# Three more groups transposed by DMA instead of TensorE, and one pair of scores placed in a later tile

## The chip, the cores and the metric

One core of a Trainium2 chip runs the whole program. The metric is the device time of one execution in microseconds (us). The kernel before took 308.35 us, the median of 3 runs (308.3 to 310.02).

## What is computed

Retention (attention without a softmax, with a decay by distance) and behind it a two-layer network with a gate:

```python
scores = scale * np.matmul(q, k.transpose(0, 1, 3, 2))        # batch 8, heads 8, sequence 576, head dim 64
gamma = 1.0 - 2.0 ** (-5.0 - np.arange(H))
Dmat = np.where(rel >= 0, gamma[:, None, None] ** rel[None, :, :], 0.0)   # rel = i - j
x = np.matmul(scores * Dmat, v)                               # then as 4608 tokens x 512
h = x @ w_in                                                  # 512 -> 2048
out = (h * np.cos(h)) @ w_out                                 # 2048 -> 512
```

## The kernel before

**Groups.** The 4608 tokens are 36 groups of 128. For each group, `load` (line 97) issues three DMAs on SP's queue (q, k, v in float32); `prep` (line 123) has POOL (GpSimd) multiply q and k by powers of the decay into the bfloat16 tile `qks`, and copy v to `vb`. The scores need q and k with the head dimension on the partitions, so `transposes` (line 147) turns `qks` into `qkT`: for groups below `N_PE_T` on TensorE (eight 128x128 transposes on line 155 into PSUM banks that it is given, then two copies by ACT on line 160), for the others by one transposing DMA on SP's queue (line 150). `scores` (line 170) makes 8 score blocks and has DVE multiply them with a triangular mask into `ret` (line 186). `state` (line 194) adds the group to a running state and copies it (line 215). `attn_out` (line 223) sums the state's part and the masked scores' part in a PSUM bank and evacuates it to the transposed activations `xT` (line 260), on DVE or on ACT as the caller says.

**Tiles.** The network works on ten tiles of 512, 256, 256 and seven times 512 tokens (n = 0 to 9). `mm1` (line 264) is the first layer with ACT's cosine (line 283; a sine with a quarter period added) and DVE's product (line 284); `mm2` (line 286) is the second layer, whose result ACT copies to `ot` (line 301) and SP stores (line 303).

**Order.** The order on each engine is the order in which the program is written, by hand. In the second layer of tile n, the list `todo` says at which step of `order` (a step is one matmul of line 292) the attention of later groups is put in: a pair (50, f) means that f is issued just before step 50. `inside` does the same within the first layer. Thus group 5 has its transposes at step 61 of tile 0 and its scores inside the first layer of tile 1; groups 6 and 7 have their transposes at steps 4 and 9 of tile 1 and their scores at step 16; the scores of groups 8 and 9 come at step 11 of tile 2, those of 10 and 11 at step 25 of tile 2, those of 12 to 15 in tile 3 at steps 12 and 25, and those of 16 and 17, the first of tile 4, at step 52 of tile 3.

**Feeding.** After each store, `feed(s)` (line 308) goes on with loads, preparations and, for groups from `N_PE_T` on, transposing DMAs, as far as the conditions on lines 312 to 323 let it. All these DMAs and the stores are issued by SP in that order, so a transposing DMA whose input isn't ready holds up what is behind it. The counters start at 6 (line 431), because groups 4 and 5 have been loaded and prepared ahead of the loop.

**PSUM.** Banks a, b and m hold 1024 float32 a partition each and are shared by transposes, scores, outputs and both layers; n and st are half as large.

Of the kernel before, what the change touches and what calls it, by code (L numbers as in the profile page):

```python
# [17 lines left out]
def kernel(  # L18
# [16 lines left out]
    nc = tc.nc  # L35
# [8 lines left out]
    NG = NTOK // P  # L44
# [8 lines left out]
    widths = [512, 256, 256] + [512] * 7  # L53
    assert sum(widths) == NTOK
    starts = [sum(widths[:n]) for n in range(len(widths))]
    N_PE_T = 8

    consts = ctx.enter_context(tc.tile_pool(name="consts", bufs=1))
    first = ctx.enter_context(tc.tile_pool(name="first", bufs=1))
# [87 lines left out]
    def transposes(g, banks=None, only=(0, 1)):  # L147
        qks, vb, qkT, qT = tiles["a", g]
        if g >= N_PE_T:
            nc.sync.dma_start(qkT, qks.rearrange("s m h d -> s (m h d)"), transpose=True)  # L150
            return
        for m in only:
            ps = psum.tile([P, HG, P], BF16, tag=banks[m], name="tr")
            for hg in range(HG):
                nc.tensor.transpose(  # L155
                    ps[:, hg, :],
                    qks[:, m, 2 * hg : 2 * hg + 2, :].rearrange("s h d -> s (h d)"),
                    ident,
                )
            nc.scalar.copy(qkT[:, m * HG : (m + 1) * HG, :], ps)  # L160
        if ("fv", g) in tiles and g != 3:
            nc.scalar.copy(vb, tiles.pop(("fv", g)))
# [60 lines left out]
    def attn_out(gs, bank, evac=nc.vector.tensor_copy):  # L223


        ps = psum.tile([P, len(gs), HG, P], F32, tag=bank, name="ov")
        for x, g in enumerate(gs):
            c = g % PER
            if c == 0:
                continue  # L230
            qT = tiles["a", g][3]
            sb = tiles.pop(("sb", g))
            n = HP if c == MIX else P
            for hg in range(HG):
                nc.tensor.matmul(  # L235
                    ps[:, x, hg, :n],
                    lhsT=sb[:, hg, :],
                    rhs=qT[:, hg, :n],
                    start=(hg == 0),
                    stop=False,  # L240
                    skip_group_check=True,
                )
        for x, g in enumerate(gs):
            vb = tiles["a", g][1]
            ret = tiles.pop(("ret", g))
            for hg in range(HG):
                for he in range(2):
                    nc.tensor.matmul(  # L248
                        ps[he * D : he * D + D, x, hg, :],
                        lhsT=vb[:, 2 * hg + he, :],  # L250
                        rhs=ret[:, he, hg, :],
                        start=(g % PER == 0 and hg == 0),
                        stop=(hg == HG - 1),
                        skip_group_check=True,
                    )
        n = max(m for m in range(len(starts)) if starts[m] <= gs[0] * P)
        if ("x", n) not in tiles:
            tiles["x", n] = xp.tile([P, DG, 512], BF16, tag="xT", name="xT")
        t0 = gs[0] * P - starts[n]
        evac(  # L260
            tiles["x", n][:, :, t0 : t0 + len(gs) * P].rearrange("p c (x i) -> p x c i", i=P), ps
        )
# [43 lines left out]
    loaded = prepared = transposed = 4  # L306

    def feed(s):

        nonlocal loaded, prepared, transposed  # L310
        while True:
            while prepared < min(loaded, NG, 2 * s + 7, s + 11):
                prep(prepared)
                prepared += 1
                if transposed < N_PE_T:
                    transposed += 1

            if N_PE_T <= transposed < min(prepared, s + 11) and (
                transposed <= loaded - 2 or loaded == NG
# [108 lines left out]
            attn_out([g], "m", evac=nc.scalar.copy)  # L428
    for g in (4, 5):
        prep(g)  # L430
    loaded = prepared = transposed = 6


    def pair(g, banks, sc, av, out=None):

        mid = (sc + av) // 2
        return [
            (sc - 5, lambda: state(g)),
            (sc, lambda: (scores(g, banks[0]), scores(g + 1, banks[1]))),
            (mid, lambda: state(g + 1)),  # L440
            (av, lambda: attn_out([g, g + 1], out or banks[0])),
        ]

    def scores2(g):
        if g < NG:
            scores(g, "a")
            scores(g + 1, "b")

    late = []
    for n, w in enumerate(widths):  # L450

        if n in (0, 3):
            halves = [(h, et) for et in range(0, ET, 4) for h in range(2)]
            if n == 3:
                halves.sort()
            blocks = [(et, half * 256, 256) for half, et in halves]
        elif n == 1:
            blocks = [(et, half * P, P) for half in range(2) for et in (0, 8)]
        else:
            blocks = [(et, 0, w) for et in range(0, ET, 1024 // w)]  # L460
        banks = {0: "abmabmab", 1: "bmba", 2: "bmab", 3: "mamabmab"}.get(n, "abmabmab")
        for i, (et, c0, cw) in enumerate(blocks):

            inside = {
                (0, 0): {2: lambda: (attn_out([3], "n"), state(3))},
                (1, 0): {4: lambda: scores(5, "a")},
                (1, 1): {3: lambda: attn_out([5], "a", evac=nc.scalar.copy)},
            }.get((n, i), {})
            mm1(n, et, c0, cw, banks[i], inside)
            if (n, i) == (3, 1):  # L470
                late.pop()()

        g = starts[n] // P + w // P
        if n == 0:
            todo = [
                (45, lambda: transposes(4, "ab")),
                (49, lambda: state(4)),
                (50, lambda: scores(4, "a")),
                (57, lambda: attn_out([4], "a")),
                (61, lambda: transposes(5, "ba")),  # L480
                (63, lambda: state(5)),
            ]
        elif n == 1:
            todo = [(4, lambda: transposes(6, "mb")), (9, lambda: transposes(7, "mb"))]
            todo += pair(6, "ab", 16, 27)
        elif n == 2:
            todo = pair(g, "ab", 11, 25, "m")
            todo += [(25, lambda: scores2(g + 2)), (29, lambda: state(g + 2))]
            late += [lambda: (state(g + 3), attn_out([g + 2, g + 3], "b"))]
        elif n + 1 < len(widths):  # L490
            todo = [
                (5, lambda: state(g)),
                (12, lambda: scores2(g)) if n == 3 else (0, lambda: None),
                (
                    25 if n == 3 else 20,
                    lambda: (
                        attn_out(
                            [g, g + 1], "m", nc.scalar.copy if n == 3 else nc.vector.tensor_copy
                        ),
                        scores2(g + 2),  # L500
                    ),
                ),
                (16, lambda: state(g + 1)),
                (36, lambda: state(g + 2)),
                (52, lambda: (attn_out([g + 2, g + 3], "m"), scores2(g + 4))),
                (45, lambda: state(g + 3)),
            ]
        else:
            todo = []
        todo.sort(key=lambda u: u[0])  # L510
        order, cols = [], [(0, DM)]
        for tsi in range(w // P):
            if (n + 1, tsi + 1) == (len(widths), w // P):
                cols = [(0, DM // 2), (DM // 2, 3 * DM // 4), (3 * DM // 4, DM)]
            order += [(tsi, et, c0, c1) for c0, c1 in cols for et in range(ET)]
        if n == 0:

            part = 3 * ET // 4
            order[: 2 * ET] = [
                (tsi, et, 0, DM)  # L520
                for tsi, et in [(t, e) for e in range(part) for t in range(2)]
                + [(t, e) for t in range(2) for e in range(part, ET)]
            ]
        for i, (tsi, et, c0, c1) in enumerate(order):
            while todo and todo[0][0] <= i:
                todo.pop(0)[1]()
            mm2(n, tsi, et, c0, c1)
        assert not todo
# [30 lines left out]
```

## Time and profile before

| | before |
|---|---|
| median of the runs | 308.35 us |
| the profiled execution | 308.27 us |
| its span | 306.3 us |
| TensorE busy (PE) | 300.5 us |
| DVE, ACT, POOL busy | 175.8, 117.2, 99.0 us |
| transposes on TensorE (line 155) | 48 matmuls, 220 ns each as listed, pipelined |
| copies behind them (ACT, line 160) | 12, 588 ns each |
| transposing DMAs | 28, 4.4 us each from issue to landing |
| TensorE's granted clock | full throughout |

The span runs from the first to the last instruction of the profiled execution; the run itself is 2.0 us longer. The busy time of PE counts pipelined matmuls from start to end, so the distance from one start to the next is what an additional matmul costs. In the lists of the profile, a tile's name stands before the arrow and what it is made from behind it: `qkT<-qks` on SP's queue (SPq) is a transposing DMA, `tr<-ident,qks` on PE is a transpose on TensorE, `sc<-qkT` are scores, `h` and `o` are the two layers, `fq`, `fk` and `fv` the loads. DMA issues are listed with the time to landing, that is until the last byte's completion is signalled.

### The profile page before, as it was taken

What the parts mean: (1) busy time and instruction counts of PE and PEld (TensorE: products, weight loads), DVE (VectorE), ACT (ScalarE), POOL (GpSimd) and SP (SyncE); (2) the same over time, 40 slices, a digit from 0 to 9 for tenths busy, and PEclk for the clock granted to TensorE, in tenths of its full rate; (3) what the DMA queues carried; (4) which work ended last, traced back from release to release, by engine and by line L of the source; (5) the groups of instructions that cost most, each with busy time, mean ns of one, the idle gap of its engine ahead of it and who ended that gap; (6) DMA issues with size and microseconds to landing.
All of it is one profiled execution on the core that took longest, in us unless ns stands there. A gap on an engine that the chain in (4) does not pass through costs nothing.

```text
span 306.3 us, 5685 instructions
## 1 busy us (share of the span) xinstructions
PE 300.5 (98%) x2361; PEld 171.2 (56%) x2361; DVE 175.8 (57%) x180; ACT 117.2 (38%) x136; POOL 99.0 (32%) x123
## 2 busy tenths in 40 slices
PE   7899999999999999999999999999999999999996
PEld 3478547757588554454545554455445544554444
DVE  5776425565777746656576556755676547624610
ACT  3566234715046223631264026411651165105611
POOL 2740066634554534544533334314430000000000
PEclk9999999999999999999999999999999999999999
DMA  8999999999999999999993999189925300010012
GB/s 210 213 211 206 205 230 229 190 198 246 164 243 208 196 253 199 268 220 205 258 205 58 223 218 225 23 190 208 243 48 77 99 35 0 36 68 34 2 68 69
DMA packets 148697, 49.65 MB, mean 162 GB/s; under 512 B 138688, under 2 KB 144192, under 8 KB 148672
## 3 DMA queue, kind: packets, MB, share of 16 engines
q1 hardware_dynamic: 144448, 45.10, 78.5%
q0 software_dynamic: 4224, 4.19, 8.2%
q8 instruction: 18, 0.29, 0.4%
q14 instruction: 7, 0.06, 0.1%
HBM read 36.70 MB, written 9.44 MB: 151 GB/s over the span
## 4 chain that ended last, share of the span: by engine, by line
PE 94%; SPq 2%; DMA 2%; DVE 0%; POOL 0%; issue 0%; ACT 0%; ACTq 0%
PE h L275 41%; PE o L292 41%; PE ov L248 3%; PE sc L177 3%; PE st L206 2%; PE ov L235 2%; DMA fk<-in_k_dram 2%; SPq L109 2%; PE tr L155 1%; PE sc L168 0%; DVE xT L260 0%; POOL qks L135 0%; SPq L336 0%; ACT ot L301 0%; ACTq L301 0%
## 5 line engine op out<-in xcount | busy, mean ns | idle before, releaser
L292 PE MATMUL o<-w_out_sb,gT 128*128 128x512 bf16 (+2 forms) x608 | 134.4, 369 | 0.0
L275 PE MATMUL h<-xT,w_in_sb 128*128 128x512 bf16 (+2 forms) x832 | 127.5, 314 | 0.1
L284 DVE TENSOR_TENSOR gT<-h,cosh 128x1024 bf16<-128x1024 f32 x72 | 88.2, 1225 | 55.9 <-ACT cosh L283 55.8
L275 PEld LDWEIGHTS <-w_in_sb 128*128 128x128 bf16 x832 | 75.8, 98 | 50.4 <-issue 0.4
L283 ACT ACTIVATE cosh<-h,half_pi 128x1024 f32<-128x1024 f32 x72 | 80.2, 1113 | 52.0 <-PE h L275 52.0
L292 PEld LDWEIGHTS <-gT 128*128 128x128 bf16 x608 | 55.3, 98 | 56.2
L134 POOL TENSOR_TENSOR qks<-fq,gq 128x512 bf16<-128x512 f32 x32 | 33.3, 1042 | 104.3 <-DMA fq<-in_q_dram 102.0
L301 ACT COPY ot<-o 128x512 f32<-128x512 f32 (+2 forms) x38 | 21.4, 563 | 115.4 <-PE o L292 115.4
L135 POOL TENSOR_TENSOR qks<-fk,gk 128x512 bf16<-128x512 f32 x35 | 36.5, 1042 | 13.1 <-DMA fk<-in_k_dram 11.4
L186 DVE TENSOR_TENSOR ret<-sc,tri 128x1024 bf16<-128x1024 f32 x32 | 38.0, 1218 | 4.6 <-PE sc L177 4.5
L215 DVE TENSOR_TENSOR sb<-st,diag_105 128x512 bf16<-128x512 f32 x32 | 22.0, 687 | 27.8 <-PE st L206 27.8
L260 DVE CAST xT<-ov 128x1024 bf16<-128x1024 f32 (+1 forms) x16 | 18.5, 1158 | 23.5 <-PE ov L248 23.5
L141 POOL CAST vb<-fv 128x512 bf16<-128x512 f32 x32 | 19.5, 610 | 7.7 <-DMA fv<-in_v_dram 5.7
L206 PEld LDWEIGHTS <-qks 128*128 128x128 bf16 (+1 forms) x128 | 9.5, 98 | 7.0 <-issue 0.4
L248 PE MATMUL ov<-ret,vb 128*64 128x128 bf16 x288 | 12.1, 223 | 0.0
L206 PE MATMUL st<-vb,qks 128*128 128x128 bf16 (+1 forms) x116 | 11.2, 220 | 0.1
L177 PEld LDWEIGHTS <-qkT 64*128 64x128 bf16 x288 | 8.1, 94 | 5.0 <-ACT qkT L160 2.3
L235 PEld LDWEIGHTS <-sb 128*128 128x128 bf16 x128 | 8.3, 98 | 3.8
L160 ACT COPY qkT<-tr 128x512 bf16<-128x512 bf16 x12 | 6.6, 588 | 9.3 <-PE tr L155 9.3
L177 PE MATMUL sc<-qkT 64*128 64x128 bf16 x256 | 10.1, 218 | 0.0
L248 PEld LDWEIGHTS <-vb 128*64 128x64 bf16 x288 | 8.7, 109 | 2.0
L235 PE MATMUL ov<-qkT,sb 128*128 128x128 bf16 (+1 forms) x116 | 8.8, 216 | 0.0
(49 smaller groups left out, 57.3 us busy)
## 6 DMA issues: line engine op xcount, KB each, us to landing
out_dram<-ot SPq DMA_DIRECT2D x35, 256.0 KB, 3.1
fk<-in_k_dram SPq DMA_DIRECT2D x32, 256.0 KB, 4.8
fv<-in_v_dram SPq DMA_DIRECT2D x32, 256.0 KB, 4.9
fq<-in_q_dram SPq DMA_DIRECT2D x28, 256.0 KB, 4.1
w_in_sb<-in_moe_w_in_dram POOLq DMA_DIRECT2D x4, 512.0 KB, 8.7
w_out_sb<-in_moe_w_out_dram POOLq DMA_DIRECT2D x4, 512.0 KB, 15.9
fq_111<-in_q_dram SPq DMA_DIRECT2D x2, 512.0 KB, 4.4
fq<-in_q_dram SPq DMA_DIRECT2D x8, 128.0 KB, 3.8
```

Source lines behind the costliest of these rows:

```text
L134: nc.gpsimd.tensor_tensor(out=qks[:, 0], in0=fq, in1=tq, op=ALU.mult)
L135: (nc.vector if g == 3 else nc.gpsimd).tensor_tensor(out=qks[:, 1], in0=fk, in1=tk, op=ALU.mult)
L177: nc.tensor.matmul(ps[:, he, hg, :], lhsT=qkT[d0 : d0 + D, HG + hg, :], rhs=qT[d0 : d0 + D, hg, :], start=True, stop=True,)
L186: nc.vector.tensor_tensor(out=ret.rearrange("p a b i -> p (a b) i"), in0=ps.rearrange("p a b i -> p (a b) i"), in1=mask.unsqueeze(1).to_br ...
L206: nc.tensor.matmul(ps[:, hg, :], lhsT=qks[p0:, 1, 2 * hg : 2 * hg + 2, :].rearrange("s h d -> s (h d)"), rhs=vs[p0:, 2 * hg : 2 * hg + 2, ...
L215: nc.vector.tensor_tensor(out=sb, in0=ps, in1=diag2.unsqueeze(1).to_broadcast([P, HG, P]), op=ALU.mult,)
L235: nc.tensor.matmul(ps[:, x, hg, :n], lhsT=sb[:, hg, :], rhs=qT[:, hg, :n], start=(hg == 0), stop=False, skip_group_check=True,)
L248: nc.tensor.matmul(ps[he * D : he * D + D, x, hg, :], lhsT=vb[:, 2 * hg + he, :], rhs=ret[:, he, hg, :], start=(g % PER == 0 and hg == 0), ...
L275: nc.tensor.matmul(ps[:, j, :], lhsT=w_in_sb[:, dg, (et + j) * P : (et + j + 1) * P], rhs=xT[:, dg, c0 : c0 + w], start=(dg == 0), stop=(d ...
L283: nc.scalar.activation(cosh, ps, ACTF.Sin, bias=half_pi, scale=1.0)
L284: nc.vector.tensor_mul(gT[:, et : et + m, c0 : c0 + w], ps, cosh)
L292: nc.tensor.matmul(ps, lhsT=gT[:, et, tsi * P : (tsi + 1) * P], rhs=w_out_sb[:, et, c0:c1], start=(et == 0), stop=(et == ET - 1),)
```

## The change

The threshold `N_PE_T` goes from 8 to 5, so that groups 5, 6 and 7 are transposed by DMA; their calls of `transposes` leave the hand-written lists, and the counter `transposed` starts at 5, so that `feed` issues the DMAs. The scores of groups 16 and 17 leave step 52 of tile 3 and come at step 12 of tile 4; the outputs of these groups, with the scores of groups 18 and 19 behind them, move from step 20 to step 25 of tile 4, and their evacuation goes from DVE to ACT. In tiles 5 to 8 all stays.

```diff
-    N_PE_T = 8
+    N_PE_T = 5
...
-    loaded = prepared = transposed = 6
+    loaded = prepared = 6
+    transposed = 5
...
                 (57, lambda: attn_out([4], "a")),
-                (61, lambda: transposes(5, "ba")),
                 (63, lambda: state(5)),
             ]
         elif n == 1:
-            todo = [(4, lambda: transposes(6, "mb")), (9, lambda: transposes(7, "mb"))]
-            todo += pair(6, "ab", 16, 27)
+            todo = pair(6, "ab", 16, 27)
...
-                (12, lambda: scores2(g)) if n == 3 else (0, lambda: None),
+                (12, lambda: scores2(g)) if n in (3, 4) else (0, lambda: None),
                 (
-                    25 if n == 3 else 20,
+                    25 if n in (3, 4) else 20,
                     lambda: (
                         attn_out(
-                            [g, g + 1], "m", nc.scalar.copy if n == 3 else nc.vector.tensor_copy
+                            [g, g + 1], "m", nc.scalar.copy if n in (3, 4) else nc.vector.tensor_copy
                         ),
                         scores2(g + 2),
                     ),
                 ),
...
-                (52, lambda: (attn_out([g + 2, g + 3], "m"), scores2(g + 4))),
+                (
+                    52,
+                    lambda: (attn_out([g + 2, g + 3], "m"), scores2(g + 4 if n > 3 else NG)),
+                ),
```

`scores2(NG)` issues nothing.

## Prediction

> **What bounds the kernel now.** I read the page first, then the chain of waits, PE's waits, the timelines of PE and SP between 40 and 120 us, and the DMA view in narrow windows.
>
> ```profile
> PE 300.5 (98%) x2361; PEld 171.2 (56%) x2361; DVE 175.8 (57%) x180; ACT 117.2 (38%) x136; POOL 99.0 (32%) x123
> ...
> DMA  8999999999999999999993999189925300010012
> ...
> PE 94%; SPq 2%; DMA 2%; DVE 0%; POOL 0%; issue 0%; ACT 0%; ACTq 0%
> PE h L275 41%; PE o L292 41%; PE ov L248 3%; PE sc L177 3%; PE st L206 2%; PE ov L235 2%; DMA fk<-in_k_dram 2%; SPq L109 2%; PE tr L155 1%; PE sc L168 0%; DVE xT L260 0%; POOL qks L135 0%; SPq L336 0%; ACT ot L301 0%; ACTq L301 0%
> ```
>
> After the first 18 us TensorE sets the end: it stands on 94% of the chain and its order of work is fixed, so a matmul taken out there shortens the span by its pitch, and a wait put there lengthens it one for one. But the DMA row is just as full up to slice 21 (about 160 us): loading runs at the engines' limit there, far ahead of need, and anything added to it delays all that follows in SP's queue.
>
> PE's timeline around the fifth group's transposes and scores (columns: start, duration, engine, line, operation, count):
>
> ```profile
> 47.72 0.61 PE L155 MATMUL tr<-ident,qks 128*128 128x128 bf16 x8
> 48.16 0.59 PE L292 MATMUL o<-w_out_sb,gT 128*128 128x512 bf16 x2
> 48.59 0.39 PE L206 MATMUL st<-vb,qks 128*128 128x128 bf16 x4
> 48.82 0.38 PE L292 MATMUL o<-w_out_sb,gT 128*128 128x512 bf16 x1
> 49.03 1.06 PE L275 MATMUL h<-xT,w_in_sb 128*128 128x128 bf16 x16
> 50.02 0.40 PE L177 MATMUL sc<-qkT 64*128 64x128 bf16 x8
> ```
>
> The next work starts 0.44 us after the eight transposes start (the 0.61 includes the last one's tail): 55 ns each, without a gap. PE's timeline at the first scores whose operands come late by DMA, groups 10 and 11:
>
> ```profile
> 81.37 0.64 PE L248 MATMUL ov<-ret,vb 128*64 128x128 bf16 x16
> 81.94 0.62 PE L177 MATMUL sc<-qkT 64*128 64x128 bf16 x16
> 82.50 1.04 PE L292 MATMUL o<-w_out_sb,gT 128*128 128x512 bf16 x4
> ```
>
> SP's own timeline (issue start and length), and what the DMA view gives for the single issues at 43.11 and 74.17 us (last column: time to landing):
>
> ```profile
> 43.11 1.57 SPq L109 DMA_DIRECT2D fv<-in_v_dram  x1
> 44.73 0.99 SPq L109 DMA_DIRECT2D fq<-in_q_dram  x1
> ...
> 74.17 2.02 SPq L150 DMA_TRANSPOSE qkT<-qks  x1
> 76.24 1.29 SPq L109 DMA_DIRECT2D fq<-in_q_dram  x2
> ```
>
> ```profile
> fv<-in_v_dram SPq DMA_DIRECT2D x1, 256.0 KB, 6.1
> ```
>
> ```profile
> qkT<-qks SPq DMA_TRANSPOSE x1, 5.0
> ```
>
> So group 6's values land at 49.2 and group 11's transpose at 79.2. The latter is wanted at 82.2 (half of the 16 score matmuls after 81.94): 3.0 us of slack.
>
> **What the Trainium skill says.** TensorE: Matmul & The Clock Gate, "Wait — 56ns, not 53.3ns?": warm matmuls of 128 columns follow each other at 55.6 ns; the trace agrees (55 ns above). DMA: Bandwidth & Descriptors, "Anatomy of one DMA": "DMA engines do not wait on semaphores"; a wait sits on the issuing sequencer, so a transposing DMA whose input isn't ready blocks SP and all behind it. The trace agrees so far as SP's waits list the transposes' line as waiting for POOL (7.8 us in 8 waits). The same page, "Latency and other measured facts", gives transposing DMAs 261 GB/s in the strided case; 262,144 bytes at that rate are an estimate of 1.0 us, and the trace's landings below agree.
>
> **The change part by part.**
>
> *Removed from PE:* 3 groups x 8 transposes x 55 ns = 1.33 us, all inside stretches where PE has no gap (47.7, 58.3 and 59.9 us). The six ACT copies (588 ns each, 3.5 us) and three PSUM evacuations go too; ACT is idle for longer than that around them, so they are worth nothing. Gain 1.33 us.
>
> *Added to SP's queue:* following the feeding loop by hand, store 0 is now followed by load 6, T5 (the transposing DMA of group 5), load 7, T6; store 1 by load 8, T7, load 9, T8; from store 2 on the order is the old one. What is an extra transpose worth while the queue is full? Landing of each transpose after the landing of the transfer ahead of it, T8 to T17: 0.86, 0.93, 0.87, 1.64, 0.84, 0.95, 0.83, 0.93, 0.95, 0.90 us, mean 0.97. A second way: q loads of full groups land 4.21 us apart without transposes (46.11 to 58.75, three groups, one store) and 5.27 with (58.75 to 79.81, four groups, two stores); less 0.12 for the store share, 0.93. The bounds: 0.83 is the least seen; the last transposes, which run nearly alone, keep the engines busy for some 1.5 us. I take 0.97, so 2.9 us for three (2.5 to 4.5). Nothing takes this back in time: between 60 and 100 us SP's waits sum to 0.6 us, and it issues without a rest until 159 us.
>
> *T5's own wait.* POOL ends group 5's k product at 44.4 and SP reaches T5's place at 44.7, so SP doesn't wait. T5 lands behind group 6's values: 49.2 + 0.97 = 50.2 (bounds 50.0 and 50.7). PE wants it at 50.02 - 0.44 = 49.58. PE waits about 0.6 us (0.4 to 1.2), with the whole first-layer work of tile 1 queued behind, and ACT's cosine and DVE's product after that. Net at this point: +0.2.
>
> *T6 and T7* land at 49.2 + 0.97 + three loads at 1.1 + 0.97 = 54.5 and about five DMAs later, 59.5. Scores 6 and 7, at 62.13 before, come at 62.13 + 0.2 - 0.89 = 61.4: two us of cover. Net -0.7.
>
> *T11.* 79.2 + 2.9 = 82.1. PE now wants it at 82.2 - 0.7 = 81.5, so scores 11 wait 0.6 us; behind them stand the last seven second-layer matmuls of tile 2 and tile 3. Net 0.0. There is a disturbance: transfers of the engines' instructions (single packets of 16 KB, 1.0 to 1.3 us, the DMA view's q8) hold a landing back by about 1 us when they fall in; one stands at 79.7 us, just behind T11 before. If it falls in front of T11 now, T11 lands at 83.2 and the net is +1.0. Taking T11 between them, a little nearer the first (82.4): net +0.3.
>
> *What is late next.* T13 before 94 (wanted 102), T15 at 104.8 (wanted 107.2): cover 2.4 us. T17 moves from 113.4 to 116.3; its scores were wanted at 115.0 and would have waited 1.3 us, but they are moved into tile 4. T19 and T21 keep over 7 us. Output tiles: the copy at 113.24 needs the store that landed at 107.4, now 110.3; covered.
>
> *The moved scores of groups 16 and 17:* 16 matmuls, 0.55 us of PE both before and after: nothing. In tile 4 they stand at step 12, about 134.8, when DVE has ended the last product of that tile (134.55) and T17 has landed for 18 us. Then 2 x 1.22 us of masks on DVE must be over by the outputs at step 25; tile 3 has this very arrangement (scores 102.46, masks to 105.27, outputs 106.06, no gap in PE), so it is covered by second-layer matmuls. If that cover were gone, DVE's lateness would go to PE in full, up to 2.4 us. The evacuation at step 25 goes from DVE (1.22 us) to ACT (1.01 us), which has only store copies then; the second masks on DVE start earlier for it. Nothing.
>
> *Sum:* -1.33 + 0.6 (T5) + about 1.0 (T11) = +0.3 us on the span of 306.3. The profiled execution took 308.27, 2.0 more than its span, and the median of the runs is 308.35; so 308.6.
>
> **Rivals.** (1) *The transfers are hidden.* T5 arrives in time and T11 too, and PE keeps 1.33 us: 307.0. For it: many DMAs land early by some tenths, and PE's shift decides. Against: it needs three transposes for at most 1.5 us, 0.5 each, where none of ten took under 0.83. (2) *Slower: a transpose in the full queue costs its price alone, 1.5 us.* Place: scores 11. T11 lands at 83.7 and PE, wanting it at 81.5, waits 2.2: +1.5, 309.9. It decides from 1.0 us a transpose on, where the two waits eat the gain. For it: the nearly lone transposes and the one landing of 1.64. Against: nine of ten were under 1.0. (3) *A late queue spreads:* at 2.1 us a transpose or more, scores 7 and 15 wait as well and T11 costs over 3.5: 311.5 and above. Nothing in the landings speaks for it. That the edit does nothing can't be: the transposes leave PE in any case.
>
> **How the numbers follow.** Forecast 0.55 (307.7 to 309.3), rival 1 0.17, rival 2 0.20, rival 3 0.08. The range reaches from rival 1 past rival 2: 306.9 to 310.3. About 1%, 3 us, is what a measurement of this kernel can tell from no change. Faster by more than that isn't to be had from 1.33 us of removed work: 0.02 for what I haven't seen. Slower takes rival 3 or the tail of rival 2: 0.09. Within: 0.89.
>
> **What would show it.** Line 155 with 24 matmuls fewer; 31 transposing DMAs; T5 landing near 50.2 with PE waiting 0.4 to 1.2 us ahead of the scores at about 50.2; T11 landing at 82.1 to 83.2 with a wait of 0.5 to 1.7 us on line 177; the store after T8 issued about 3 us later than 59.71; no PE gap in tile 4. I am wrong if T5 lands before 49.6, T11 before 81.5 or after 84, or if PE waits elsewhere.

## The result, and the profile after

The changed kernel took 312.54 us (median of 6 runs, 311.5 to 314.59) against 308.33 before (also 6 runs): 1.0139 times as long, 95% interval 1.0097 to 1.0181. That is outside the predicted range of 306.9 to 310.3. Two later measurements of the same kernel on other occasions gave 1.0096 (1.0064 to 1.0128) and 1.0060 (1.0029 to 1.0091); the last corresponds to 310.2 us, inside the predicted range. The ratios leave out executions more than 1.5% above the fastest of the same kernel, the medians and ranges keep them. The changed kernel scatters far more than the kernel before: 16 of its 30 executions on the three occasions show a mean granted clock of 0.995 or less, of the kernel before 2 of 126. The profiled execution is one of the longer ones, 314.14 us with a span of 312.4, 6.1 more than before.

The page after, lines as shown of before, and the row of the granted clock:

```profile
PE 299.9 (96%) x2304; PEld 171.5 (55%) x2337; DVE 174.9 (56%) x179; ACT 115.0 (37%) x131; POOL 99.1 (32%) x123
...
PEclk9999999999869999999999999999999999999999
DMA  8999999999999999999994799559952310010012
...
PE 78%; DMA 11%; SPq 6%; issue 1%; POOL 1%; ACT 0%; DVE 0%; ACTq 0%
PE h L275 36%; PE o L292 34%; SPq L109 5%; DMA w_out_sb<-in_moe_w_out_dram 5%; DMA qkT<-qks 4%; PE ov L248 3%; PE sc L177 3%; PE ov L235 2%; PE st L206 2%; DMA fk<-in_k_dram 2%; DMA fq<-in_q_dram 1%; POOL w_in_sb L376 1%; DVE xT L260 0%; SPq L303 0%; ACT cosh L283 0%
```

Two things are new: the chain runs through `DMA qkT<-qks`, back along SP's queue as far as the weights, and TensorE's granted clock, full throughout before, dips in two slices. PE's waits after name the place:

```profile
PE sc L177 <- DMA qkT<-qks: 3.8, 2, 3.1
```

Its timeline shows the first of the two waits, ahead of the scores of group 5 (the last column is the idle time before, and what ended it), and the second, ahead of those of group 11, with what follows:

```profile
48.59 1.06 PE L275 MATMUL h<-xT,w_in_sb 128*128 128x128 bf16 x16
50.34 0.40 PE L177 MATMUL sc<-qkT 64*128 64x128 bf16 x8 [0.69 <-DMA qkT<-qks]
...
81.37 0.40 PE L177 MATMUL sc<-qkT 64*128 64x128 bf16 x8
84.87 0.61 PE L177 MATMUL sc<-qkT 64*128 64x128 bf16 x8 [3.10 <-DMA qkT<-qks]
85.81 1.49 PE L292 MATMUL o<-w_out_sb,gT 128*128 128x512 bf16 x3 [0.33 <-issue]
```

The 16 scores that stood together before (81.94) are torn apart: those of group 10 run at 81.37, those of group 11 wait until 84.87. The transposing DMA on which they wait was issued at 78.06, and the DMA view of that issue gives 6.8 us to landing, where group 11's took 5.0 before:

```profile
qkT<-qks SPq DMA_TRANSPOSE x1, 6.8
```

And after the wait everything is slow: three matmuls of 512 columns take 1.49 us together, where four took 1.04 before (82.50, in the prediction). The idle time "issue" behind the scores is no wait: the trace has six of the seven matmuls that stand there, so one record is missing. Busy times by stretch, first after, then before (columns: stretch, length, busy time and count of PE, PEld, DVE, ACT and POOL, granted clock, DMA share, GB/s):

```profile
84.20:91.00 6.80, 5.80 (x29) 3.40 (x31) 1.92 (x2) 0.59 (x1) 3.25 (x4) 0.50 1.26 193
```

```profile
84.20:91.00 6.80, 6.80 (x79) 6.00 (x78) 5.08 (x7) 2.81 (x3) 4.02 (x6) 1.00 1.17 244
```

For 6.8 us (84.2 to 91.0) TensorE was granted half its clock. The counts, 29 matmuls and 79, aren't for the same work: in the changed kernel the first 0.67 us are still the wait, and the kernel before is already further on, at shorter matmuls.

Following the same instruction through both timelines gives the account (a wait costs a little more than its idle time, because the last matmul before it runs out first). Scores 5 start at 50.34 (before 50.02): 0.44 us of removed transposes and 0.76 lost waiting. Scores 6 start at 61.56 (62.13): another 0.89 saved, net -0.57, and the same at scores 10 (81.37, 81.94). Scores 11 start at 84.87 where they would have started at 81.59: 3.3 us lost, net +2.7. The outputs in tile 3 start at 94.14 (88.50): net +5.6, so the half clock cost 2.9 us. To the last matmul 0.1 more comes in, and 0.4 at the very end of the program (last section). The sum: -1.33 + 0.76 + 3.3 + 2.9 + 0.1 + 0.4 = +6.1.

### The profile page after: what moved, and what is told of

Its sections match the earlier page's. It is cut to its first block, busy times and chain, and to the rows that moved or that the text cites. A ratio compares the mean times of both kernels' runs of the same rounds, so it can differ in the third digit from the quotient of the medians.

```text
span 312.4 us, 5604 instructions
## 1 busy us (share of the span) xinstructions
PE 299.9 (96%) x2304; PEld 171.5 (55%) x2337; DVE 174.9 (56%) x179; ACT 115.0 (37%) x131; POOL 99.1 (32%) x123
## 4 chain that ended last, share of the span: by engine, by line
PE 78%; DMA 11%; SPq 6%; issue 1%; POOL 1%; ACT 0%; DVE 0%; ACTq 0%
PE h L275 36%; PE o L292 34%; SPq L109 5%; DMA w_out_sb<-in_moe_w_out_dram 5%; DMA qkT<-qks 4%; PE ov L248 3%; PE sc L177 3%; PE ov L235 2%; PE st L206 2%; DMA fk<-in_k_dram 2%; DMA fq<-in_q_dram 1%; POOL w_in_sb L376 1%; DVE xT L260 0%; SPq L303 0%; ACT cosh L283 0%
## 5 line engine op out<-in xcount | busy, mean ns | idle before, releaser
L292 PE MATMUL o<-w_out_sb,gT 128*128 128x512 bf16 (+2 forms) x583 | 131.9, 370 | 2.5 <-issue 1.8
L275 PEld LDWEIGHTS <-w_in_sb 128*128 128x128 bf16 x832 | 76.6, 99 | 51.1 <-issue 1.0
L260 DVE CAST xT<-ov 128x1024 bf16<-128x1024 f32 (+1 forms) x15 | 17.3, 1153 | 20.9 <-PE ov L248 20.9
L260 ACT CAST xT<-ov 128x512 bf16<-128x512 f32 (+1 forms) x6 | 4.4, 728 | 7.1 <-PE ov L248 7.0
```

The lines of the kernel that those rows point to most:

```text
L275: nc.tensor.matmul(ps[:, j, :], lhsT=w_in_sb[:, dg, (et + j) * P : (et + j + 1) * P], rhs=xT[:, dg, c0 : c0 + w], start=(dg == 0), stop=(d ...
L292: nc.tensor.matmul(ps, lhsT=gT[:, et, tsi * P : (tsi + 1) * P], rhs=w_out_sb[:, et, c0:c1], start=(et == 0), stop=(et == ET - 1),)
```

## The experiments

In what follows T5 to T17 are the transposing DMAs of these groups. "Theory" is that the added DMAs hold up T11 in SP's full queue, and that PE's wait for it costs twice, as time and as clock. "The rival" of an experiment is the one named in its expectation.

**1. The move alone.** All transposes on TensorE, the scores of groups 16 and 17 in tile 4:

```diff
-    N_PE_T = 5
+    N_PE_T = 8
...
-    loaded = prepared = 6
-    transposed = 5
+    loaded = prepared = transposed = 6
...
+                (61, lambda: transposes(5, "ba")),
...
-            todo = pair(6, "ab", 16, 27)
+            todo = [(4, lambda: transposes(6, "mb")), (9, lambda: transposes(7, "mb"))]
+            todo += pair(6, "ab", 16, 27)
```

> The scores of groups 16 and 17 move into tile 4 with the outputs behind them, and all transposes of groups 5 to 7 stay on TensorE. Queue theory (the added DMAs delay the eleventh group's transpose, PE waits, and the long wait halves the clock): the move plays no part, 308.3 us, between 307.8 and 308.9, no new wait on PE, clock 1.000. Rival, that the new place of these scores costs time in tiles 3 and 4: at least 2 us of the 4.2 show here, 310.3 or more.

Measured: 308.42 us, 0.9994 (0.9982 to 1.0007). PE waits for no DMA of attention, the clock is 1.0. The move by itself costs nothing that the times can tell (0.1 us in the timeline of tile 4); the rival falls.

**2. The DMA part alone.** The kernel before with only the threshold, the counters and the removed calls of the change:

```diff
-    N_PE_T = 8
+    N_PE_T = 5
...
-    loaded = prepared = transposed = 6
+    loaded = prepared = 6
+    transposed = 5
```

and without the three calls of `transposes`.

> Groups 5 to 7 are transposed by DMA, the scores of groups 16 and 17 stay in tile 3. Queue theory: the wait at the scores of group 11 and the halved clock come as in the changed kernel, 311.5 to 314.5; after that PE is so late that the scores of group 17 find their transpose landed, so leaving out the move costs nothing. Rival (the move costs): under 310.5.

Measured: 310.45 us, 1.0048 (1.0018 to 1.0079), under the expected range: the profiled execution waited only 0.58 us at scores 11 and kept its clock, so PE came to scores 17 early enough to wait there too (1.2 us). By its own sign (under 310.5) this run speaks for the rival, by 0.05 us; experiment 1 has already ruled the rival out. The loss is in this part, but its size changes from run to run, from 309.04 to 314.2.

**3. and 4. Two groups, or one, by DMA.** As changed, but with `N_PE_T` 6 (group 5 on TensorE again) or 7 (groups 5 and 6, with group 6's call of `transposes` back in tile 1):

```diff
-    N_PE_T = 5
+    N_PE_T = 6
...
-    loaded = prepared = 6
-    transposed = 5
+    loaded = prepared = transposed = 6
...
+                (61, lambda: transposes(5, "ba")),
```

> Only groups 6 and 7 by DMA, group 5 on TensorE again; the move stays. Queue theory: group 11's transpose lands 1.2 to 1.5 us earlier than with three, at 83.3 to 83.6; PE wants it at 81.4 and waits 1.9 to 2.2 us, too short to lose the clock: 309.4 to 309.8. Rival, that the wait for group 5's transpose and what follows in tile 1 carries the loss: no loss here, 307.4 (the 0.9 us of removed transposes).

> Only group 7 by DMA; the move stays. Queue theory: group 11's transpose lands at 80.4 to 81.5, PE wants it at 81.8: no wait, 0.45 us of transposes saved, 307.9. If a DMA added to the full queue costs PE time in itself, whatever waits: about a third of the loss, 309.7.

Measured: 308.08 us for two, 0.9989 (0.9971 to 1.0008), and 308.42 for one, 0.9997 (0.9984 to 1.0010). With two, T11 was issued at 75.31 and landed 5.3 us later, at 80.6, ahead of PE's 81.4; PE's waits no longer list it, and are those of before:

```profile
PE idle L168 <- DVE zeros L356: 1.3, 1, 1.3
PE tr L155 <- POOL qks L135: 0.6, 2, 0.4
PE tr L398 <- DVE qs L387: 0.5, 1, 0.5
PE sc L177 <- ACT qkT L160: 0.2, 1, 0.2
```

My expectation of a wait of two us with two DMAs was wrong: T11 came 1.4 us later than before, not 4. With one DMA it landed at 80.5, hardly earlier, so its lateness isn't a fixed price times the number of DMAs. There is a step between two and three: as long as T11 lands ahead of PE the delay costs nothing. (One of the 20 runs with two took 311.33 us at a clock of 0.994; perhaps it reached the step, but it has no trace.) The savings of 0.45 and 0.9 us aren't seen in full because the end of the program takes 0.4 us longer.

**5. The wait filled.** The changed kernel, with 14 matmuls on zeros ahead of scores 11 (`warm`, line 164, through the argument `idle` of `scores`):

```diff
-            todo += [(25, lambda: scores2(g + 2)), (29, lambda: state(g + 2))]
+            todo += [
+                (25, lambda: (scores(g + 2, "a"), scores(g + 3, "b", idle=14))),
+                (29, lambda: state(g + 2)),
+            ]
```

It ran beside the changed kernel unaltered:

> The changed kernel itself once more, on the chip of the three that follow. The wait at the scores of group 11 comes in every run, 1 to 3.3 us by how the transfers fall: 310.5 to 313 us; a granted clock under 0.997 only in runs over 311.5.

> The changed kernel with 14 idle matmuls of 512 columns put ahead of the scores of group 11 (3.0 us of PE at 216 ns each; they compute nothing that is used). Theory (the wait is filled, so that PE doesn't go idle there and the clock isn't lost, and the arrival of the transpose no longer matters): before less 1.33, plus 0.75 for group 5's wait, plus 3.0, plus 0.4 at the end of the program, 311.2 us, scatter under 0.5, clock 0.999 or more in all runs. Rival, that the clock falls by something else than PE's idleness (the load of the DMA engines, or the change's other parts): clocks of 0.995 and less appear as in the changed kernel.

Measured: the changed kernel 311.88 us (309.54 to 314.26, 9 runs), the filled one 311.94 (311.5 to 312.34, 4 runs). The medians are alike, the spread isn't: of the nine unaltered runs five had a clock of 0.989 to 0.994, and these are the five longest (311.88 and more); of the four filled ones none was under 0.999. The filled kernel missed its expectation by 0.7 us and scattered a little more (0.8 us) than the 0.5 expected, because T11 was later still than the filling reached. T11 landed late again in the filled one's profile (85.7), and PE still waited a little, at full clock:

```profile
82.12 3.19 PE L168 MATMUL sc<-zeros 128*128 128x512 bf16 x13
85.79 0.40 PE L177 MATMUL sc<-qkT 64*128 64x128 bf16 x8 [0.47 <-DMA qkT<-qks]
86.11 1.04 PE L292 MATMUL o<-w_out_sb,gT 128*128 128x512 bf16 x4
```

Four matmuls of 512 columns in 1.04 us here, three in 1.49 after the empty wait. So it is PE's idleness that takes the clock. Four runs are no large sample, but the other runs agree.

In the four kernels where the wait for T11 is filled or its reader stands later (experiments 5, 6, 7 and 10) none of 37 executions had a clock under 0.998, though T11 was late in all four profiles (83.2 to 85.7). In experiments 2 and 12, where the wait is as in the changed kernel, 5 of 21 fell to 0.994 or less. And the profile of experiment 11 lost its clock in the first tile, where no transposing DMA is in flight: PE idled 2.11 us for weights and then 2.58 us for DVE, and the stretch from 21.92 to 28.75 was granted half the clock:

```profile
20.42 1.05 PE L275 MATMUL h<-xT,w_in_sb 128*128 128x256 bf16 x8 [2.11 <-DMA w_in_sb<-in_moe_w_in_dram]
24.27 0.64 PE L248 MATMUL ov<-ret,vb 128*64 128x128 bf16 x8 [2.58 <-DVE vb L427]
```

```profile
21.92:28.75 6.83, 4.47 (x29) 3.31 (x30) 2.12 (x4) 1.11 (x1) 0.00 (x0) 0.50 1.24 206
```

**6. and 7. Scores 11 later, then three of them.** The changed kernel with scores 11 inside the second block of tile 3; in the second kernel scores 5 and 15 later too:

```diff
-            todo += [(25, lambda: scores2(g + 2)), (29, lambda: state(g + 2))]
+            todo += [(25, lambda: scores(g + 2, "a")), (29, lambda: state(g + 2))]
...
+                (3, 1): {2: lambda: scores(11, "b")},
...
-            if (n, i) == (3, 1):
+            if (n, i) == (3, 2):
```

> The changed kernel with the scores of group 11 taken from step 25 of tile 2 into the second block of tile 3's first layer (some 4.5 us later), and the outputs of groups 10 and 11 one block later. Theory (that one wait and its clock are the loss): what is left is the wait at group 5, the 1.33 us saved and 0.4 at the end: 308.2 us, between 307.7 and 308.9, clock 0.999 or more. Rival (a late queue costs wherever it first meets PE): the wait moves to the scores of group 15, and the time stays over 310.

> As the last, with the scores of group 5 three sub-blocks later in tile 1 (0.7 us, its outputs as much later) and those of group 15 at step 34 of tile 3. Theory: no wait is left but a few tenths at group 5: 307.5 us, between 307.2 and 307.9, faster than before. If the saved transposes are worth nothing even without waits: 308.3 or more.

Measured: 310.89 us, 1.0079 (1.0067 to 1.0091), and 310.01, 1.0066 (1.0046 to 1.0085). Both miss. The waits for T11 are gone and every clock is 0.999 or more, so that part holds; but the edit made waits of its own. PE's timeline of the first (tile 3's third and fifth block):

```profile
88.60 1.91 PE L275 MATMUL h<-xT,w_in_sb 128*128 128x256 bf16 x16 [0.28 <-DVE gT L284]
...
94.70 0.49 PE L275 MATMUL h<-xT,w_in_sb 128*128 128x256 bf16 x3 [1.10 <-DVE xT L260]
```

With the outputs of groups 10 and 11 one block later, DVE evacuates them too late for the block that needs them. Between the first store of tile 2 and tile 3's fifth block both profiles lose 1.9 us against the kernel before. With the 1.33 saved, the 0.4 at the end of the program and 0.2 of small losses, that is an estimate of 309.7 for the second kernel, from the 308.56 that the kernel before took on this occasion, and of 310.4 for the first, which also keeps T5's wait. The first one's own profile has 1.5 us more, from a wait for weights in the first tile that the edit doesn't touch. The rival (the wait moves to scores 15) isn't borne out either: they don't wait.

**8. and 9. The queue alone.** The kernel before, all transposes on TensorE, and three more DMAs at the places of T5, T6 and T7, from the same `qks` into scrap that nobody reads:

```diff
                 load(loaded)
                 loaded += 1
+                if loaded in (7, 8, 9):
+                    r = 2 * (loaded % 2)
+                    spare = qs4[:, r : r + 2].rearrange("p r h d -> p (r h d)")
+                    qks = tiles["a", loaded - 2][0].rearrange("s m h d -> s (m h d)")
+                    nc.sync.dma_start(
+                        spare.rearrange("p (a b) -> p a b", b=P), qks, transpose=True
+                    )
```

In the second, `nc.sync.dma_start(spare, qks)`, a plain copy.

> The kernel before, with all its transposes on TensorE, and three more transposing DMAs at the places of T5, T6 and T7 in SP's queue, whose results nobody reads. Theory (what counts is the time they take in the full queue, not that anyone waits for their data): group 8's transpose lands 3.5 to 4.8 us later than before, group 11's 3.5 to 5.6 (82.7 to 84.8); PE, which wants group 11's at 82.2, waits 0.5 to 2.6 us, and for group 17's up to 1.5: 309.5 to 312. Rival (PE loses by waiting for the data of groups 5 to 7, and the queue makes up for them later): 308.3 to 308.9.

> As the last, but the three extra DMAs are plain copies of the same 256 KB from SBUF to SBUF, in packets of 2 KB and not 256 bytes. If the number of small packets is what a transpose costs: about the price of a store, 0.75 us each, group 8's transpose 2.3 us late, group 11's at 81.5, no wait: 308.3 to 309. If the bytes or the place in the queue are: as with the transposes, 309.5 to 312.

Measured: 310.49 us, 1.0085 (1.0061 to 1.0109), with transposing DMAs; 309.77, 1.0049 (1.0030 to 1.0068), with copies (four runs each). T11 landed at 84.4 (issued 77.27, 7.2 us) and at 83.4 (issued 76.61, 6.8), after 79.2 before. Nobody waits for the scrap; PE does the same work as before and stops at the same place. PE's timeline with the transposing ones, then the stretch behind it (the profiled execution is the longest of the four, 312.58 us; the other three took 310.4 to 310.6 and kept the clock):

```profile
84.48 0.60 PE L177 MATMUL sc<-qkT 64*128 64x128 bf16 x8 [2.15 <-DMA qkT<-qks]
85.01 1.46 PE L292 MATMUL o<-w_out_sb,gT 128*128 128x512 bf16 x3
```

```profile
84.60:87.90 3.30, 3.30 (x18) 1.53 (x15) 1.76 (x2) 0.00 (x0) 1.46 (x2) 0.50 1.38 169
```

This shows the queue, without the data, to be the cause: 4 to 5 us of delay at T11 from three DMAs, and the half clock once the wait is long enough (2.15 us here, for 3.4 us). The wait of 1.9 to 2.2 us that experiment 3 expected to be too short for that would thus not have been safe. Transposing makes it dearer than copying the same bytes (T8 landed 5.4 us late against 3.2), but the greater part is there with copies in eight times larger packets (2 KB), so the small packets aren't the main cause.

**10. The rearrangement mended.** Scores 5 and 11 later, the state of group 11 where it was, and its outputs evacuated by ACT:

```diff
-                (1, 0): {4: lambda: scores(5, "a")},
-                (1, 1): {3: lambda: attn_out([5], "a", evac=nc.scalar.copy)},
+                (1, 0): {7: lambda: scores(5, "a")},
+                (1, 1): {6: lambda: attn_out([5], "a", evac=nc.scalar.copy)},
+                (3, 1): {2: lambda: scores(11, "b")},
...
-            if (n, i) == (3, 1):
-                late.pop()()
+            if (n, i) in ((3, 1), (3, 2)):
+                late.pop(0)()
...
-            todo += [(25, lambda: scores2(g + 2)), (29, lambda: state(g + 2))]
+            todo += [(25, lambda: scores(g + 2, "a")), (29, lambda: state(g + 2))]
-            late += [lambda: (state(g + 3), attn_out([g + 2, g + 3], "b"))]
+            late += [
+                lambda: state(g + 3),
+                lambda: attn_out([g + 2, g + 3], "b", evac=nc.scalar.copy),
+            ]
```

> The changed kernel with the scores of groups 5 and 11 later as in the runs before, those of group 15 in their old place, and the outputs of groups 10 and 11 evacuated by ACT one block later, so that the two waits that the first rearrangement made (0.28 and 1.1 us ahead of tile 3's third and fifth block) shrink to one of 0.1. Theory: 1.33 saved, 0.1 lost at group 5, 0.1 in tile 3, up to 0.3 at group 15, 0.4 at the program's end: 307.7 us, between 307.3 and 308.2. If a later queue still finds a wait: 308.5 or more.

Measured: 308.54 us (22 runs), 1.0010 (1.0000 to 1.0021). PE's waits hold 0.5 us for transposes in all, and the profile has T11 landing at 85.4, later than in the changed kernel's own. The change's loss is gone while the late queue is still there: the loss was where scores 11 stood. But nothing is gained over the kernel before, 0.8 us more than expected: in the profile the 1.33 us saved go in some 0.4 each at scores 5, in tile 3, at scores 15 and at the end of the program.

**11. and 12. The change beside its DMA part.**

> The changed kernel, on the same chip and in turn with the next one, which leaves the move out. If the move pays (the scores of group 17 would wait for their transpose in tile 3): 0.5 to 1.5 us faster than the next. If PE's lateness has already covered that wait, or the move costs something: the same within 0.5, or slower.

> Groups 5 to 7 by DMA, the scores of groups 16 and 17 in tile 3 as before the change. With the wait of 1.2 us that the first run of this kernel showed at the scores of group 17: slower than the changed kernel by 0.5 to 1.5 us, 311.5 to 313. Otherwise equal or faster.

Measured on one chip: 310.51 us, 1.0060 (1.0029 to 1.0091), with the move and 310.59, 1.0088 (1.0053 to 1.0124), without. The profile with the move was disturbed in the first tile (experiment 5 shows where) and isn't used for the comparison. The intervals overlap, so whether the move pays isn't settled. Its reason is real: without it PE waited at scores 17 in both profiles (1.2 and 0.46 us), with it in no profile.

No version ran faster than the kernel before by more than the measurement can tell; the nearest is the one with two groups by DMA.

## Why the prediction was wrong

**The gain** was right: 24 transposes, 0.44 us a group, 1.33 in all, can be followed through the timelines.

**T5's own wait** was right: 50.2 was predicted, it landed at 50.3 (50.1 to 51.1 in the other profiles), and PE lost 0.76 us of the 0.4 to 1.2 allowed. In another profile of the same kernel it idled 1.4 us there.

**The places** were right: the second wait is at scores 11, T6, T7 and T15 find cover, the move is free but for 0.1 us. (The six ACT copies are themselves the PSUM evacuations that the prediction counts beside them; nothing rests on it.)

**The step that failed first is "Added to SP's queue"**, 0.97 us for a DMA, 2.9 for three, at most 4.5. T8 landed at 66.4 against 61.7 before, 1.6 us for each, and T11 at 84.8 against 79.2, 5.6 us late. T8 on SP's queue and its time to landing, after, then before:

```profile
61.13 2.42 SPq L150 DMA_TRANSPOSE qkT<-qks  x1
qkT<-qks SPq DMA_TRANSPOSE x1, 5.3
```

```profile
56.60 3.01 SPq L150 DMA_TRANSPOSE qkT<-qks  x1
qkT<-qks SPq DMA_TRANSPOSE x1, 5.1
```

In the seven other profiles that have all three DMAs and PE's transposes removed (that of experiment 11, late from the start, apart) T8 was 4.3 to 5.5 us late, and T11 landed between 82.4 and 85.7. In four of them T11 came by 83.2, within what was predicted; the late T8 had by then been made good in part, which the prediction ruled out.

Both my ways to 0.97 were too short. The first took the landing of each transpose behind the transfer ahead of it. That is indeed 0.7 to 0.95 us for T5, T6 and T7, 2.6 of T8's 4.8; but the transfers behind them come later as well, 2.1 us in sum, half of it at group 9's k and v. SP's issue of a transposing DMA lasts 2.1 to 3.6 us in this stretch (44 to 80 us), of a load 0.4 to 1.2. The estimate of 1.0 us that the prediction worked out from a bandwidth fell short in the same way.

While T7 was in flight the engines moved next to nothing for a microsecond (last two columns: share, counted where a packet starts, and GB/s):

```profile
58.00:59.00 1.00, 1.00 (x5) 0.49 (x5) 0.57 (x1) 1.00 (x1) 0.00 (x0) 1.00 2.88 133
59.00:60.00 1.00, 1.00 (x7) 0.45 (x5) 0.87 (x1) 0.10 (x1) 0.73 (x1) 1.00 0.08 16
```

They weren't empty: the trace's packet records have some twenty packets of 256 bytes there that took 1.4 to 1.6 us each, where the mean is about 0.02. The same is seen during T5 (47.2 to 49.2), and during the first transposing DMAs of the kernel before (59.7 to 60.7, 65.6 to 67.6). In the run with plain copies in the places of T5 to T7 there is none ahead of T8. So an added transposing DMA can hold the engines up beyond its own bytes; what makes the packets stand still, and how much of the 2.1 us is due to it, stays open.

The second way, by whole groups, ended its last interval on the first half of group 13's q, which comes in two DMAs; with the second half (80.5) it gives 1.1, not 0.93. The changed kernel itself, from group 6's to group 11's q (46.1 to 74.1, five groups with a transpose each), gives 5.6 us a group where groups without one took 4.2: some 1.3 us for each after the stores are taken off. At T8 one, two and three added DMAs cost 1.6, 2.6 and 4.8 us.

The rest at T11 goes with the instruction transfers, which I had put at 1 us: the trace has them at 81.1 and 82.6, and T11 landed 3.2 us behind the transfer ahead of it (1.6 before). That the two together caused this is inferred from their place.

**The second failed step is one that isn't there**: I took a wait to cost its own length ("a wait put there lengthens it one for one"). Waits of 2.15 and 3.1 us were followed by half clock for 3.4 and 6.8 us, which cost 1.6 and 2.9 us more; waits of 0.2 to 1.4 us weren't.

The Trainium skill has this, in TensorE: Matmul & The Clock Gate, "What's actually happening": the clock falls to half after at least one idle window of about 3.4 us, and the windows run freely, without regard to when the kernel starts. The half clocks here last one and two such windows (3.4 and 6.8 us), in agreement; but idle times of 2.15 and 3.1 us, shorter than a window, were enough here, and there the measurement decides.

Rival 2 (1.5 us a transpose, the wait at scores 11, 309.9) had the queue's price nearest and lacked only the clock. Rival 3 came nearest to the result in time (311.5 and above), yet its mechanism, a lateness spread over scores 7 and 15, isn't what happened.

So the mechanism of the forecast was right as far as it went, the size of one term too small, and what a long wait adds wasn't in it. The range was too narrow for that: between a wait of one and of three us lies a step in the clock.

## What to carry to other kernels

Work moved from a full engine to a queue that is just as full isn't free just because it runs ahead of need. Ask which transfer behind it has the least slack (here 3.0 us), and price the added one by how far whole groups move apart, not by its own landing. Keep waits on TensorE short: two of about one us cost two, one of three cost six. Where a transfer can't be earlier, moving its first reader later, and with it the evacuation that this delays, removes the loss (308.54 against 310.5 to 312.5).

## What the runs showed of the hardware that I had not expected

- Instruction transfers of 16 KB, single packets of 0.9 to 1.7 us on one DMA engine, seem to hold back the transfer in flight by about 1 us or more. Such packets, or smaller ones of 8 KB, fall into T11's flight in every profile; T11 landed 1.6 to 1.8 us behind the transfer ahead of it in most, 2.6 in one and 3.2 in three, where most other transposing DMAs landed 0.7 to 1.0 behind. With T11 near its limit this is probably much of the scatter between runs; no experiment tests it.
- At its end the program waits for the completion of all DMAs in a fixed order of their semaphores. If the last store's stands early in that order, the remaining waits come after it: in all kernels with one to three added DMAs 2.8 to 2.9 us pass from the start of the last store's issue to the end, in the two without 2.5. Experiment 4 saved 0.45 us of transposes and lost them there.
- Idle matmuls in a wait that can't be avoided kept the clock in all of four runs: at equal medians they took the spread from 4.7 to 0.8 us.
- In the 3.4 us ahead of each of the three half clocks seen (from 84.19 after, 84.52 in experiment 8, 21.92 in experiment 11) PE was idle for 2.4, 2.2 and 2.1 us in sum. No wait of up to 1.4 us led to one; where between them the limit lies isn't measured.
